# First attention pair loaded as f32 by two other queues, shorter VectorE steps, whole-array summary scores, and a planner with measured times

## The chip, the cores and the metric

The kernel runs on one core of one Trainium2 chip. The core has five engines with instruction streams of their own: TensorE (PE, its weight loads are shown as PEld), VectorE (DVE), ScalarE (ACT), GpSimd (POOL) and SyncE (SP), and 16 DMA engines that all of the core's queues share. Matrix products are written to PSUM, which has eight banks; everything else lies in SBUF. The time that counts is the device time of one execution in microseconds, median of the runs. In the lines of the profile, L12 means line 12 of the kernel before.

## What is computed

Two stages follow each other. The first is a sparse attention with 4 batches, 8 heads, 768 positions and head size 64: each query sees the keys less than 16 positions away, and 24 summaries of blocks of 32 keys.

```python
k_sum = k.reshape(B, H, nb, block, D).max(axis=3)      # block = 32, nb = 24
v_sum = v.reshape(B, H, nb, block, D).mean(axis=3)
scores_l = where(|i - j| < 16, scale * q @ k.T, -1e9)
scores_s = scale * q @ k_sum.T + log(block)
a = softmax(concat[scores_l, scores_s]);  x = a @ concat[v, v_sum]
```

The second is a mixture of 8 experts over the 3072 rows of x (512 wide), hidden size 1024. The gate's weights P are normalised eight times by rows and by columns over all rows, and the output is the sum of the experts weighted by P.

```python
P = exp(x @ w_gate - max)
for _ in range(8):
    P /= P.sum(1, keepdims=True) + 1e-9
    P /= P.sum(0, keepdims=True) + 1e-9
    P *= N / E
out = sum_e P[:, e:e+1] * (relu(x @ w1[e]) @ w2[e])
```

## The kernel before, in words

**Tiling.** Attention works on 16 pairs of heads, four pairs to a batch. Pair i belongs to batch i // 4. The two heads of a pair lie on partitions 0 to 63 and 64 to 127 of the transposed tiles `kT` and `qT`. Batch 0 is done in halves of 384 positions (`pair_half`), the other batches as whole pairs (`pair_whole`). For each pair: keys, queries and values are loaded by POOL's queue with a cast to bf16 (`load_qk`, `load_qh`, `load_v`); keys and queries are transposed on PE (`tr`, `tr_qh`, L312 to L315 and L299) and copied out of PSUM by ACT or DVE (L204); from pair 12 on the transposes are DMAs on SP's queue (`tr_dma`, L320). `key_max` (L338) takes the maxima of 32 keys, `block_sums` (L354) the sums of values by a product with the constant `m_blk`, and `block_out` (L361) copies them into the diagonal blocks of `V_s` or `V_e`. `scores` and `scores_h` (L344) make the local scores, `summaries` and `summaries2` (L432, L442) the summary scores, as products of 64 rows and 32 columns, one per head. ACT takes exponentials (L389, L452, L469), DVE multiplies by the band mask, PE makes the weighted values (L418 to L424, L492 to L507), DVE divides by the sums (`normalize`, L520 and L521), and `to_xT` or, for pairs 10 to 14, a DMA transpose (`x_dma`, L324) brings the result into `xT`. `near_values` copies edge rows of the values by four small DMAs on SP's queue.

**Expert 0** is computed in eight parts of 384 rows as soon as its rows of `xT` and its weights are there (L208 `hidden_mm`, L218 `project_mm`). It fills the time that attention leaves on PE. Experts 1 to 7 come after it in an order written out by hand (the loop over `groups`, from L1217), which the change does not touch.

**What sets the order.** For attention, expert 0, the gate's eight turns (`bridge`, L1120) and the first four groups of expert 1, a planner writes the order. Each step is a `Unit` with an engine (or a choice of two), a cost in us, the steps it depends on, a priority, and PSUM buffers that it opens or uses. `Plan.order` (L58) keeps a clock per engine, adds `HOP` (0.15) between engines and `RESHAPE` (0.1) when PE's tile shape changes, and emits the step that can start first. PSUM banks of a kind ("m" three, "a" three, "s" one double bank) are taken in turn, as a ring. A step's `lag` is the time after its end until others may use it; loads and DMA transposes have planned lags. Where the plan leaves PE idle before the first evacuation of expert 0, it inserts filler products of zeros (`keep_busy`, L566). The plan decides the order of instructions alone; on the chip each engine runs its list in order and waits on semaphores.

**At the front**: POOL's queue issues pair 0's keys, queries and values, makes the identity, issues pair 1's keys and queries, makes the band mask (two operations that wait for DVE's memset of `band`, L585), and goes on with pair 1's values, pairs 2 and 3, expert 0's weights and the later batches. DVE sets the constants (`constants`, L595) meanwhile; `pads` (L589) clears the gaps in the tiles `Eh`.

Of the kernel before, what the change touches and what calls it, by code (L numbers as in the profile page):

```python
# [34 lines left out]
class Plan:  # L35

    HOP = 0.15
    RESHAPE = 0.1

    def __init__(self, slots, idle=None):  # L40
        self.slots, self.idle, self.shape = {}, idle, None
        self.ring, self.turn, self.free, self.waiting = {}, {}, {}, []
        self.more(slots)

    def more(self, slots):
        for t, n in slots.items():
            self.slots[t], self.ring[t], self.turn[t] = n, [None] * n, 0
# [10 lines left out]
    def order(self):  # L58
        free, ring, turn, waiting = self.free, self.ring, self.turn, self.waiting
        left = []  # L60

        def ready(u):
            t = 0.0
            for i, b in enumerate(u.opens):
                old = ring[b.tag][(turn[b.tag] + i) % self.slots[b.tag]]
                if old is not None:
                    if any(x.start is None for x in old.users):
                        return None
                    t = max([t] + [x.end + (self.HOP if x.on not in u.eng else 0.0) for x in old.users])
            return t  # L70

        while waiting or left:
# [4 lines left out]
            for u in left:  # L77
# [3 lines left out]
                for e, cost in u.eng.items():  # L81
                    if e == "PE" and u.shape != self.shape:
                        cost += self.RESHAPE
                    t = max([t0, free.get(e, 0.0)]
                            + [d.end + d.lag + (self.HOP if d.on != e else 0.0) for d in u.deps])
# [8 lines left out]
            if self.idle is not None:  # L94
# [3 lines left out]
                while self.idle is not None and t > free.get("PE", t) + us:  # L98
# [10 lines left out]
                    ring["m"][turn["m"] % self.slots["m"]] = x.opens[0]  # L109
                    turn["m"] += 1  # L110
                    yield x
            u.start, u.end, u.on = t, end, e
# [3 lines left out]
            for b in u.opens:  # L116
                ring[b.tag][turn[b.tag] % self.slots[b.tag]] = b
                turn[b.tag] += 1
            left.remove(u)
            yield u  # L120
# [3 lines left out]
def kernel(  # L124
# [23 lines left out]
    W = 16  # L148
# [86 lines left out]
    if True:  # L235
# [4 lines left out]
        m_blk = attn.tile([128, G, 128], BF16, name="m_blk")  # L240
        qT = [attn.tile([128, W + S + W], BF16, name=f"qT{i}") for i in range(NB)]
        kT = [attn.tile([128, S], BF16, name=f"kT{i}") for i in range(NB)]
        ksT = [attn.tile([128, 32], BF16, name=f"ksT{i}") for i in range(NB)]
# [14 lines left out]
        def bank(tag, name, dtype=FP32):  # L258
            pool, n = (mps, 3) if tag == "m" else (aps, NA)
            return pool.tile([128, 2048 // mybir.dt.size(dtype)], dtype, tag=tag, name=name, bufs=n)  # L260

        def banks2(name, dtype=FP32):
            return aps.tile([128, 2, 2048 // mybir.dt.size(dtype)], dtype, tag="s", name=name, bufs=NS)
# [1056 lines left out]
```

## Time and profile before

| what | value |
|---|---|
| median of 3 runs | 676.51 us (675.13 to 679.61) |
| the profiled execution's own time | 676.52 us |
| its span in the profile | 674.8 us |
| PE busy | 660.7 us (98%), 5107 matmuls |
| DVE busy | 578.9 us (86%) |
| ACT busy | 404.6 us (60%) |
| POOL busy | 132.6 us (20%) |
| granted TensorE clock | 0.999 |
| chain that ended last | PE 88%, DMA 5%, DVE 4% |

The profile is one execution. Busy is the time in which an engine had an instruction in work; matmuls are pipelined, so that a busy PE can still be waiting a little between them. Besides the page, the trace behind it can be asked for the instructions of a stretch in order of time, for busy time by stretch, for the waits and what ended them, and for the chain of work that ended last, followed back from the last instruction.

### The profile page before, as it was taken

The numbers are of one execution on the slowest core, as the hardware profiler recorded it, in microseconds if no ns is written. First come the engines' busy times: TensorE is split into PE (matmuls) and PEld (weight loads), VectorE is DVE, ScalarE is ACT, GpSimd is POOL, SyncE is SP. The second block draws the span as 40 slices with busy tenths as digits, with TensorE's granted clock in tenths as the row PEclk, the third lists the DMA queues.
The fourth block names the chain that finished last, engine by engine and source line by source line (L and its number), as shares of the span: only waits on it lengthen the run. The fifth ranks groups of instructions, "written<-read, shape, count | busy, mean of one in ns | idle before, by whom it ended". The sixth has DMA issues, their size and how long they took to land.

```text
span 674.8 us, 13527 instructions
## 1 busy us (share of the span) xinstructions
PE 660.7 (98%) x5107; PEld 434.0 (64%) x5107; DVE 578.9 (86%) x1434; ACT 404.6 (60%) x787; POOL 132.6 (20%) x177
## 2 busy tenths in 40 slices
PE   8899998999999999999999999999999999999996
PEld 4566655555666666666666666666666666666665
DVE  7778896776799988998799988998899879998885
ACT  5678885565777765555655565555555565556551
POOL 8599631121101010201010010101020101100001
PEclk9999999999999999999999999999999999999999
DMA  9999999000513050311422051306031232201224
GB/s 119 187 145 146 135 117 154 1 1 1 79 11 37 1 79 1 36 13 23 57 23 27 1 78 11 39 1 79 1 34 16 25 55 23 26 1 53 88 80 157
DMA packets 124018, 36.46 MB, mean 54 GB/s; under 512 B 110384, under 2 KB 121136, under 8 KB 123952
## 3 DMA queue, kind: packets, MB, share of 16 engines
q0 software_dynamic: 104672, 26.22, 43.4%
q1 hardware_dynamic: 18464, 8.83, 6.7%
q8 instruction: 40, 0.66, 0.4%
q10 hardware_dynamic: 816, 0.54, 0.2%
q14 instruction: 26, 0.21, 0.1%
HBM read 52.45 MB, written 6.29 MB: 87 GB/s over the span
## 4 chain that ended last, share of the span: by engine, by line
PE 88%; DMA 5%; DVE 4%; POOL 1%; issue 1%; ACT 0%; DVEq 0%; ACTq 0%
PE xy L939 36%; PE pg L933 16%; PE pb L933 11%; PE pa L933 10%; PE yps L218 5%; PE hps L208 4%; DMA xT<-xs 2%; DMA qst<-in_q_dram 2%; DMA w<-in_moe_w_dram 1%; PE sg L344 1%; PE tkq L315 1%; DVE xs L521 1%; PE vs L354 1%; PE tx L528 0%; DVE hf L883 0%
## 5 line engine op out<-in xcount | busy, mean ns | idle before, releaser
L939 PEld LDWEIGHTS <-hf 128*128 128x128 f16 x2352 | 230.1, 98 | 96.9 <-issue 2.3
L939 PE MATMUL xy<-w,hf 128*128 128x256 f16 x1312 | 183.4, 273 | 0.1
L939 PE MATMUL xy<-ws,hf 128*128 128x256 f16 x984 | 147.6, 273 | 0.4
L199 ACT ACTIVATE hf<-pg 128x512 f16<-128x512 f32 x84 | 50.2, 597 | 150.4 <-PE pg L933 150.4
L1075 DVE SCALAR_TENSOR_TENSOR out_acc<-xy,P_sb,out_acc 128x512 f32<-128x512 f32 x164 | 115.0, 742 | 1.7 <-PE xy L939 1.7
L880 DVE TENSOR_TENSOR hf<-hf 128x512 f16<-128x512 f16 x252 | 99.8, 423 | 8.8
L933 PE MATMUL pa<-xT,w 128*128 128x512 f16 x336 | 99.9, 379 | 0.0
L933 PEld LDWEIGHTS <-w 128*128 128x128 f16 x672 | 65.8, 98 | 43.8 <-issue 0.2
L883 DVE TENSOR_TENSOR hf<-pb,c 128x512 f16<-128x512 f32 x84 | 58.1, 691 | 38.8 <-PE pb L933 35.0
L184 POOL DMA_DIRECT2D w<-in_moe_w_dram x56 | 41.7, 756 | 221.1 <-PE pg L933 192.4
L933 PEld LDWEIGHTS <-ws 128*128 128x128 f16 x504 | 49.3, 98 | 25.3
L967 ACT COPY c<-pg 128x512 f32<-128x512 f32 x84 | 49.3, 586 | 22.4 <-PE pg L933 22.4
L883 DVE TENSOR_TENSOR hf<-pg,c 128x512 f16<-128x512 f32 x84 | 57.1, 679 | 0.7 <-PE pg L933 0.7
L952 ACT COPY pg<-pa 128x512 f32<-128x512 f32 x84 | 47.9, 570 | 4.8
L199 ACT ACTIVATE hf<-pa 128x512 f16<-128x512 f32 x84 | 50.6, 602 | 0.0
L960 ACT COPY c<-pb 128x512 f32<-128x512 f32 x84 | 49.7, 592 | 0.7 <-PE pb L933 0.5
L933 PE MATMUL pg<-xTs,w 128*128 128x512 f16 x168 | 50.0, 379 | 0.1
L933 PE MATMUL pg<-xTs,ws 128*128 128x512 f16 x168 | 50.0, 379 | 0.0
L933 PE MATMUL pb<-xT,ws 128*128 128x512 f16 x168 | 50.0, 379 | 0.0
L933 PE MATMUL pg<-xT,w 128*128 128x512 f16 x168 | 50.0, 379 | 0.0
L933 PE MATMUL pb<-xTs,ws 128*128 128x512 f16 x168 | 50.0, 379 | 0.0
L208 PE MATMUL hps<-xT,w 128*128 128x384 f16 x256 | 48.9, 326 | 0.0
(143 smaller groups left out, 819.6 us busy)
## 6 DMA issues: line engine op xcount, KB each, us to landing
w<-in_moe_w_dram POOLq DMA_DIRECT2D x8, 1024.0 KB, 9.0
w<-in_moe_w_dram POOLq DMA_DIRECT2D x56, 128.0 KB, 3.6
out_dram<-out_acc SPq DMA_DIRECT2D x20, 256.0 KB, 2.0
qst<-in_q_dram POOLq DMA_DIRECT2D x32, 96.0 KB, 6.0
vx<-in_v_dram POOLq DMA_DIRECT2D x16, 192.0 KB, 6.6
kst<-in_k_dram POOLq DMA_DIRECT2D x24, 96.0 KB, 6.2
w<-in_moe_w_dram POOLq DMA_DIRECT2D x2, 512.0 KB, 8.7
kst<-in_k_dram POOLq DMA_DIRECT2D x4, 192.0 KB, 4.9
```

Source lines behind the costliest of these rows:

```text
L184: nc.gpsimd.dma_start(out=t[:, :, h, :], in_=moe_w1[e].rearrange("(dk p) f -> p dk f", p=128)[:, :, f:f + 128])
L199: nc.scalar.activation(out=out, in_=in_, func=AF.Relu, bias=0.0, scale=1.0)
L208: nc.tensor.matmul(hp[:, 0:n], lhsT=w1s[e][:, dk, 128 * f:128 * (f + 1)], rhs=xT[:, dk, t0:t0 + n], start=(dk == 0), stop=(dk == KD - 1))
L218: nc.tensor.matmul(yp[:], lhsT=h[:, f, c * 128:(c + 1) * 128], rhs=w2s[e][:, f, :], start=(f == 0), stop=(f == KF - 1))
L880: nc.vector.tensor_tensor(out=out, in0=in0, in1=in1, op=ALU.subtract)
L883: nc.vector.tensor_tensor(out=out, in0=in0, in1=in1, op=ALU.add)
L933: nc.tensor.matmul(bank[:], lhsT=w[:, dk, :], rhs=x[:, dk, :], start=start and dk == 0, stop=dk == KH - 1, skip_group_check=True)
L939: nc.tensor.matmul(bank, lhsT=a(f)[:, 128 * c:128 * (c + 1)], rhs=w[:, f, :], start=start and f == 0, stop=f == FH - 1, skip_group_check=True)
L952: nc.scalar.copy(out=B["g"][:], in_=B["a"][:])
L960: nc.scalar.copy(out=B["c5"][:], in_=B["b"][:])
L967: nc.scalar.copy(out=B["c2"][:], in_=B["g"][:])
L1075: nc.vector.scalar_tensor_tensor(out=acc, in0=src, scalar=P_sb[:, t, e:e + 1], in1=acc, op0=ALU.mult, op1=ALU.add)
```

## The change

- **Pair 0's keys and first query half** are loaded as f32 by two queues other than POOL's: keys of head 0 and the queries by SP's, keys of head 1 by ACT's (`first_f32`), into tiles that later hold exponentials. ACT and DVE cast them to bf16 (`first_k`, `first_q`). POOL's queue starts with the identity and pair 0's values.
- **Constants**: the band's memset moves to the front of DVE's list, the Es tiles are cleared by ACT, `m_blk` is one shifted window of 148 columns instead of six blocks of 128, the V_s memsets are regrouped, the casts of the identity and the gate's weights come after pair 0's key maxima (`gate_constants`). A constant `own` holds ones where a head's own partitions are. The pads of the second and third Eh tile come later.
- **key_max** takes the maximum of two halves twice (32 to 16 to 8), reduces the rest, and multiplies by `own` into a block-diagonal `ksT` of 128 columns. **block_out** is one product with `own` instead of two copies.
- **Summary scores** are one product on 128 rows and 128 columns per half, for both heads, instead of one of 64 rows and 32 columns per head; `summaries2` goes.
- **Planner**: a bank is taken from those that are free first, not in turn; the time between engines is 0.23 after PE and 0.1 otherwise; costs and lags have new values.

The diff, cut to its core:

```diff
-    HOP = 0.15
+    HOP = {"PE": 0.23}
...
         def ready(u):
-            t = 0.0
-            for i, b in enumerate(u.opens):
-                old = ring[b.tag][(turn[b.tag] + i) % self.slots[b.tag]]
-                if old is not None:
-                    if any(x.start is None for x in old.users):
-                        return None
-                    t = max([t] + [x.end + (self.HOP if x.on not in u.eng else 0.0) for x in old.users])
+            t, u.slots = 0.0, []
+            for b in u.opens:
+                at = []
+                for n, old in enumerate(ring[b.tag]):
+                    if (b.tag, n) in u.slots or old is not None and any(x.start is None for x in old.users):
+                        continue
+                    at.append((max([0.0] + [x.end + hop(x, "PE") for x in old.users]) if old else 0.0, n))
+                if not at:
+                    return None
+                t0, n = min(at)
+                u.slots.append((b.tag, n))
+                t = max(t, t0)
             return t
...
-        ksT = [attn.tile([128, 32], BF16, name=f"ksT{i}") for i in range(NB)]
+        ksT = [attn.tile([128, 128], BF16, name=f"ksT{i}") for i in range(NB)]
+        own = attn.tile([128, 2, 26], BF16, name="own")
...
+        def first_f32():
+            at["kf"] = attn.tile([128, 2, 2 * LIVE * G // 4], FP32, tag="er", name="kf", bufs=2)
+            at["qf"] = attn.tile([128, 2, G * 64], FP32, tag="em", name="qf", bufs=2)
+            rows = k[0, 0:2].rearrange("j (p g) d -> p j (g d)", g=G)
+            for j, eng in ((0, nc.sync), (1, nc.scalar)):
+                eng.dma_start(out=at["kf"][:, j, 0:G * D], in_=rows[:, j, :])
+            nc.sync.dma_start(out=at["qf"][:, :, 0:HG * D],
+                              in_=q[0, 0:2, 0:HS].rearrange("j (p g) d -> p j (g d)", g=HG))
...
+        def first_k(eng, j):
+            copy(eng, at["st", 0, 0][:, j].rearrange("p g d -> p (g d)"), at["kf"][:, j, 0:G * D])
+
+        def first_q(eng):
+            copy(eng, at["st", 0, 1][:, 0].rearrange("p j g d -> p j (g d)"), at.pop("qf")[:, :, 0:HG * D])
+            at.pop("kf")
...
         def key_max(i):
             r = i % NB
-            nc.vector.tensor_reduce(out=ksT[r][:, 0:24],
-                                    in_=kT[r][:].rearrange("p (n w) -> p n w", w=32),
-                                    axis=AX.X, op=ALU.max)
+            km = attn.tile([128, 1, 24], BF16, tag="km", name="km", bufs=2)
+            half = attn.tile([128, 24, 16], BF16, tag="kh", name="kh", bufs=1)
+            rows = kT[r][:].rearrange("p (n w) -> p n w", w=32)
+            nc.vector.tensor_tensor(out=half[:], in0=rows[:, :, 0:16], in1=rows[:, :, 16:32], op=ALU.max)
+            nc.vector.tensor_tensor(out=half[:, :, 0:8], in0=half[:, :, 0:8], in1=half[:, :, 8:16], op=ALU.max)
+            nc.vector.tensor_reduce(out=km[:, 0, :], in_=half[:, :, 0:8], axis=AX.X, op=ALU.max)
+            nc.vector.tensor_tensor(out=ksT[r][:, 0:64].rearrange("p (j n) -> p j n", j=2)[:, :, 0:24],
+                                    in0=km[:].to_broadcast([128, 2, 24]), in1=own[:, :, 0:24], op=ALU.mult)
...
-            for j in range(2):
-                nc.vector.tensor_copy(out=dst[32 * j:32 * j + 32, j * VD:j * VD + D],
-                                      in_=vs[32 * j:32 * j + 32, j * D:(j + 1) * D])
+            nc.vector.tensor_tensor(
+                out=dst[0:64].rearrange("p (j x) -> p j x", j=2)[:, :, 0:D],
+                in0=vs[0:64].rearrange("p (j d) -> p j d", j=2),
+                in1=own[0:64, :, 24:25].to_broadcast([64, 2, D]), op=ALU.mult)
...
-            for j in range(2):
-                p0 = 64 * j
-                nc.tensor.matmul(ss[32 * j:32 * j + 32, 0:HS], lhsT=ksT[r][p0:p0 + 64, :],
-                                 rhs=qT[r][p0:p0 + 64, W + h * HS:W + (h + 1) * HS],
-                                 start=True, stop=True)
+            nc.tensor.matmul(ss[:, 0:HS], lhsT=ksT[r][:], rhs=qT[r][:, W + h * HS:W + (h + 1) * HS],
+                             start=True, stop=True)
...
-        nc.vector.memset(zeros, 0.0)
-        nc.vector.memset(ident, 0.0)
-        keep_busy(10)
+        nc.vector.memset(ident, 0.0)
+        nc.vector.memset(zeros, 0.0)
+        first_f32()
+        keep_busy(8)
...
             for t in E_s:
-                nc.vector.memset(t[64:128, :, :], 0.0)
+                nc.scalar.copy(out=t[64:128, :, :], in_=zeros[64:128, None, :].to_broadcast([64, HG, 128]))
...
-            U[key] = add("LAND", 0, None, [last[1]], lag=0.4)
+            U[key] = add("LAND", 0, None, [last[1]], lag=1.0 if late else 0.4)
...
-                                                        [U["kq"[z], i]] + (war_k, war_q)[z], prio, lag=5.0)
+                                                        [U["kq"[z], i]] + (war_k, war_q)[z], prio, lag=5.5)
...
-            clear = add("DVE", 0.65, lambda: pads(n), [c0], prio - 0.5) if 0 < n < NEH else None
+            clear = add("DVE", 0.65, lambda: pads(n), [U["km", n - 1]], prio - 0.2) if 0 < n < NEH else None
...
             U["near", i] = add("SP", 2.5, lambda: near_values(i), [U["v", i], U.get(("A", i - NE, 1))], prio,
-                               lag=1.9)
+                               lag=4.5)
...
                 U["xt", i] = U["x", i] = add("SP", 1.25, lambda: x_dma(i), [U["no", i, 0], U["no", i, 1]], prio,
-                                             lag=4.5)
+                                             lag=6.5)
...
-        load_pair(0, "k0v")
         U["ident"] = last[0] = add("POOL", 0.35, ident_constant, [last[0]])
+        c0 = add("DVE", 3.1, constants, [], -5.0)
+        kf = add("LAND", 0, None, [], lag=4.0)
+        qf = add("LAND", 0, None, [], lag=4.5)
+        kc = [add("ACT", 0.46, lambda: first_k("ACT", 0), [kf], -4.0), add("DVE", 0.46, lambda: first_k("DVE", 1), [kf, c0], -4.0)]
+        U["k", 0] = add("LAND", 0, None, kc)
+        U["q", 0, 0] = add({"ACT": 0.46, "DVE": 0.46}, 0, lambda: first_q(U["q", 0, 0].on), [qf, c0, *kc], -4.0)
+        load_pair(0, "v")
         load_pair(1, "k0")
...
-                    step = add(eng, us, fn, [step], -50.0, opens=o, uses=w, lag=(1.2 if n else 2.0) if fn is columns else 0.0)
+                    step = add(eng, us, fn, [step], -50.0, opens=o, uses=w, lag=0.7 if fn is columns else 0.0)
```

Most other changed lines are planned costs: 0.95 to 0.85 for `key_max`, 0.36 to 0.24 and 0.84 to 0.70 for `block_out`, 0.4 to 0.5 (batch 0) and 0.335 for the transposes, 0.22 and 0.18 to 0.17 for the summary scores, and similar small steps. As built, PE's list has 5107 matmuls before and 30 fewer after (32 summary products for 64, 24 fillers for 22).

## The prediction

> **What bounds the kernel now.** I read the busy time by stage first, cut where the work changes: attention of batch 0 (0 to 35 us), attention of batches 1 to 3 over expert 0 (to 120), the eight normalisation turns of the gate over the rest of expert 0 and the first groups of expert 1 (to 172.8). The columns are the stretch, its length, then busy time of PE, PEld, DVE, ACT and POOL, the granted clock, DMA share and GB/s.
>
> ```profile
> core 0: us, PE busy (x) PEld busy (x) DVE busy (x) ACT busy (x) POOL busy (x), PEclk, DMA share, GB/s
> 0.00:10.00 10.00, 7.53 (x67) 3.50 (x67) 7.44 (x66) 3.77 (x5) 8.06 (x16) 1.00 1.00 93
> 10.00:20.00 10.00, 9.03 (x161) 6.13 (x156) 8.78 (x23) 7.47 (x11) 9.02 (x12) 1.00 1.60 165
> 20.00:35.00 15.00, 13.14 (x192) 8.40 (x189) 10.80 (x34) 9.46 (x17) 8.47 (x10) 1.00 1.71 185
> 35.00:100.00 65.00, 64.85 (x771) 40.40 (x770) 57.03 (x153) 53.28 (x85) 47.08 (x59) 1.00 2.09 136
> 100.00:120.00 20.00, 17.41 (x187) 10.25 (x188) 14.54 (x46) 10.39 (x20) 3.44 (x5) 1.00 1.37 137
> 120.00:172.80 52.80, 52.80 (x304) 28.23 (x302) 36.52 (x92) 31.73 (x63) 13.16 (x19) 1.00 0.04 4
> ```
>
> PE is full from 35 to 100 us and from 120 on. It is empty for 35 - 29.70 = 5.30 us of the first 35 and for 20 - 17.41 = 2.59 us between 100 and 120. Part of the "busy" of the first 35 us is filler. The same view for the filler line alone (stretch, length, PE busy):
>
> ```profile
> 0.00:10.00 10.00, 5.44 (x15) 1.60 (x15) 1.00 1.00 93
> 10.00:20.00 10.00, 1.68 (x6) 0.52 (x7) 1.00 1.60 165
> 20.00:35.00 15.00, 0.49 (x2) 0.00 (x0) 1.00 1.71 185
> ```
>
> So of 172.8 us, at most 5.30 + 7.61 + 0.15 + 2.59 = 15.7 us are not useful PE work. Everything behind 172.8 us (502 us) stands in the same order in both programs: PE's last 3481 matmuls are the same. The change can win only from these 15.7 us and from the length of its own matmuls, and a microsecond won early reaches the end whole, because expert 0 fills every later gap. What holds the two weak stages is in the chain of work (start, length, what) and in the list of waits (total, times, longest):
>
> ```profile
> 7.18 0.99 POOL vx L284
> ...
> 12.94 7.66 DMA w<-in_moe_w_dram
> ...
> 22.50 11.39 DMA qst<-in_q_dram
> ...
> 101.33 15.10 DMA xT<-xs x2
> ```
> ```profile
> PE lp L542 <- DMA xT<-xs: 1.6, 1, 1.6
> ...
> PE sg L344 <- DVE qT L204: 1.0, 1, 1.0
> ...
> PE tx L528 <- DVE xs L521: 0.7, 2, 0.4
> ```
>
> Early it is the loads on POOL's queue, up to pair 4's queries (issued 21.7, used 34.03); late it is the transposes by DMA.
>
> **Part 1, loads of pair 0.** Two issues leave the head of POOL's queue: 0.95 (keys, at 1.29) and 0.74 us (queries). The wait of the band mask goes too:
>
> ```profile
> 6.48 0.31 POOL L577 TENSOR_SCALAR_AFFINE_SELECT band<-band 128x160 bf16<-128x160 bf16 x1 [0.69 <-DVE band L585]
> ```
>
> Its memset now stands at the front of DVE's constants. By the durations of the same rows (identity 0.33, values 1.04, keys and queries 0.74 each, masks 0.69, from 1.29 on) the second values issue moves from 7.12 to about 4.85: 2.3 us. The bytes are as many as before, and the DMA share is over 1.3 from 10 us on, so issuing earlier helps only if the engines had room. They had: the share in the first 5 us is 0.50. I bound what reaches pair 4 by 0 and 2.3 us. The Trainium skill (DMA: Bandwidth & Descriptors, Issuing engines are not separate DMA queues) says that transfers of all issuing engines run on the same 16 engines and interleave, so that spreading them saves issue time alone. By that rule 1.7 us of issue would be the most. The share of 0.50 speaks against reading it as "nothing"; from 10 us on the trace agrees with it.
>
> Pair 0 itself is not sooner. The f32 transfers should be there by about 3.5 us (the 256 KB stores on SP land 2.0 us after issue, the 16 KB gate weights 1.9). But half of the keys is cast on DVE behind the constants. Those run from 1.32 to 5.45 now; the new list loses 0.56 (Es), 0.28 (m_blk's size), 0.3 (four memsets) and about 0.5 (gaps between memsets of one tile) and gains 0.19 (band), 0.34 (whole ksT) and 0.35 (own): it ends near 4.7. With a cast of 0.5 (qT copy 128x384: 0.53) the transposes start near 5.2, against 5.18. DVE is what is late next. SP has nothing else before 35.9 us, so its two issues delay nobody; ACT's cast, query cast and two Es copies (four of some 0.48) fall into its idle 2.99 us before 5.75.
>
> **Part 2, DVE of batch 0.** DVE is busy 13.93 us of 5 to 21.4, so its order is the engine chain there. Query copy 0 waits behind pads and band until 6.97; in the new order it is next after the cast. The scores then wait for ACT's key copy (5.75 + 0.80) and start near 6.6 instead of 7.52. The pads (0.6) and the gate casts (0.48) now stand before the first masks, which start near 8.8 instead of 9.30. So 0.5 to 0.9 us there. Per pair, block_out changes from two casts of 0.214 to one product; the nearest rows are 0.19 (32x80) and 0.25 on the line from 0.167 (32 elements) to 0.549 (768): 0.2 us less. key_max (0.947) becomes four instructions. On the same line: 384 elements 0.35, 192 elements 0.25, a 192-element reduce 0.34, a small product 0.17: 1.11. Consecutive DVE starts overlap by some 0.08 (0.28 us instructions every 0.20), so 0.85; ends 0.85 and 1.11, which is -0.1 to +0.17 per pair. I take -0.1, nearest to the overlapped rows. By pair 3 that is 0.5 to 0.9 plus 3 x 0.3, about 1.5 us. In the later stages DVE's gain lies beside a full PE and is worth nothing.
>
> Loads allow up to 2.3, DVE about 1.5; both are needed, so I take **-1.5** (from 0 to -2.3).
>
> **Part 3, new lags and banks.** The waits of 100 to 120 us are 1.57 (logits of batch 2 for a DMA transpose), 0.40 + 0.35 (transposes waiting for normalize, itself 1.85 behind a DMA transpose) and 0.27 (near rows): 2.59. The planner counted 1.25 + 4.5 for an x transpose; the trace has a median of 6.8 to landing, highest 7.9. It now counts 7.75. In the new order 68 + 48 matmuls of expert 0 stand between the second and third logits instead of 60 + 32. At 0.163 and 0.216 (0.65 and 0.86 for four) that is 4.8 us more cover against a wait of 1.57. Free choice of banks can only remove planned waits, but the rebuilt order may meet new ones. Bounds: -2.59 and +1; I take **-2.0**.
>
> **Part 4, summary scores.**
>
> ```profile
> 39.41 0.27 PE ss L442 x4
> ...
> 34.53 0.65 PE hps L208 x4
> ```
>
> Four tiled matmuls of 384 columns take 0.27; two whole ones by the second row 0.33. Twelve pairs: +0.7. Batch 0: eight times 0.163 for about 0.24, -0.6, but half of them beside filler or idle PE, so -0.3. Sum **+0.4** (0 to +0.9). The Trainium skill (TensorEngine Tiling (Array Packing), Key Properties) says that a change of tiling mode drains the array; no row shows a drain by itself, and by it the +0.4 would shrink.
>
> Two fillers fewer ahead cost nothing: they end at about 4.5 instead of 4.7, ahead of transposes that wait until 5.2.
>
> **Sum**: 676.52 (own time of the profiled run: span 674.8 and 1.7 around it; the median of the runs is 676.51) - 1.5 - 2.0 + 0.4 = **673.4 us**. The three runs lie between 675.13 and 679.61, so about 1% is what can be told from no change.
>
> **Rivals.**
> *Nothing comes through.* The transfers share their engines (the rule of the page cited in Part 1, read strictly), pair 4's queries land at 34 us as before, and the new order trades one wait for another: 676.5 + 0.4 = 676.9. For it: DMA share of 1.6 and 1.7 from 10 to 35 us. Against it: half-empty DMA engines up to 5 us, and 2.59 us of waits with a named cause.
> *Slower: the gate's turns run out of cover.* Behind the last logits the new order leaves 88 + 72 matmuls of expert 0 instead of 96 + 88, 4.8 us less. Between successive column totals PE has 4.6 to 5.9 us of work (mean 5.1), where the totals now come every 5.79 us (126.38 to 166.90). From one total to the end of the next column sums the trace has 3.2 to 4.5 us, so the cover just suffices. It decides from a turn of about 4.6 on: if DVE's queue lets a turn take 5.8, PE waits 7 x 0.7 = 4.8 us: 678.2.
> *More.* The load stream comes through whole (-2.3), all waits of 100 to 120 go (-2.6), matmuls cost nothing, and planned bank waits of about 1 us go: 670.6.
>
> **Chances.** Forecast 0.52, nothing 0.22 (676.9), slower 0.13 (678.2), more 0.13 (670.6). Range 670.5 to 678.3: it takes in all four. Faster by over 1% (below 669.7) needs more than every term's far end: 0.05. Slower by over 1% (above 683.3) needs turns of 6.5 us or a new wait of 10: 0.07. Within 1%: 0.88.
>
> **What would show it.** Right: second values issue near 4.9, first transposes near 5.2, first scores near 6.6, pair 4's query transposes near 32.3, PE over 19 of 20 us between 100 and 120, first product of expert 1's second layer some 3 us sooner, an identical course behind it. Wrong: pair 4 at 34 again, PE waits at the gate's totals, or the PE gaps of 100 to 120 merely moved.

## The result, and the profile after

| | kernel before | changed kernel |
|---|---|---|
| median of 10 executions each | 676.57 us (675.13 to 679.61) | 671.46 us (670.13 to 674.88) |
| ratio of the times | 1 | 0.9925, 95% interval 0.9908 to 0.9942 |
| profiled execution's own time, its span | 676.52, 674.8 us | 674.88, 673.2 us |
| first product of expert 1's second layer | 168.77 us | 168.53 us |

The changed kernel is 5.1 us faster by the medians, 0.75%, where -3.1 was forecast; it lies inside the range and inside 1%. The profiled execution of the changed kernel happened to be the longest of its ten, 3.4 us above their median, and this must be kept in mind while reading its profile: some 4.5 us of it belong to an event that most executions don't have, or have smaller. A second series of the same kernel gave 672.35 us, 3.8 us below the kernel before in that series (676.18). Differences below about 1 us between two series are therefore not told apart here.

Busy time by stage in the changed kernel, with the same cuts and columns as before (stretch, length, then busy time of PE, PEld, DVE, ACT and POOL, granted clock, DMA share, GB/s):

```profile
core 0: us, PE busy (x) PEld busy (x) DVE busy (x) ACT busy (x) POOL busy (x), PEclk, DMA share, GB/s
0.00:10.00 10.00, 8.23 (x74) 3.71 (x75) 7.22 (x67) 6.22 (x10) 8.95 (x17) 1.00 1.22 151
10.00:20.00 10.00, 9.48 (x157) 6.26 (x154) 9.49 (x34) 6.15 (x9) 7.33 (x10) 1.00 1.63 178
20.00:35.00 15.00, 14.88 (x234) 10.81 (x232) 12.46 (x38) 11.60 (x21) 9.99 (x13) 1.00 1.84 180
35.00:100.00 65.00, 64.27 (x714) 40.06 (x711) 57.94 (x174) 46.28 (x76) 46.38 (x59) 1.00 1.88 134
100.00:120.00 20.00, 16.86 (x164) 9.98 (x163) 15.18 (x51) 9.60 (x18) 1.36 (x2) 0.93 1.15 126
120.00:172.80 52.80, 52.80 (x312) 28.68 (x310) 35.72 (x90) 32.06 (x62) 12.12 (x19) 1.00 0.04 5
```

The filler line alone (stretch, length, PE busy, PEld busy):

```profile
0.00:10.00 10.00, 5.81 (x14) 1.53 (x14) 1.00 1.22 151
10.00:20.00 10.00, 3.15 (x10) 0.81 (x10) 1.00 1.63 178
20.00:35.00 15.00, 0.00 (x0) 0.00 (x0) 1.00 1.84 180
```

Three things stand in these rows. From 20 to 35 us PE went from 13.14 busy us to 14.88, none of it filler: the early stage is where the gain is. Up to 20 us busy time without filler is 8.75 us now and was 9.44: nothing was won there by this measure. And from 100 to 120 us, where 19 of 20 busy us were forecast, PE has 16.86, less than the 17.41 of before, at a mean clock of 0.93.

The chain of work that ended last (start, length, what) shows both stages:

```profile
1.46 5.31 DMA vx<-in_v_dram
6.81 0.50 PE vs L393 x6
7.32 0.35 PE sg L383 x8
...
8.79 0.66 DVE Eh L503
...
31.47 0.34 PE tkq L349 x6
...
33.28 0.34 PE tkq L349 x6
...
104.56 11.35 DMA Ve<-vx
115.91 0.14 issue
116.04 0.40 PE av L464 x3
```

In the kernel before pair 4's keys and queries (the products `tkq` near 33 us) came after waits for their loads, at 32.73 and 34.03 (start, length, engine, line, operation, and in brackets the idle time before it and what ended it):

```profile
32.73 0.49 PE L315 MATMUL tkq<-ident,kst 128*128 128x128 bf16 x6 [0.46 <-DMA kst<-in_k_dram]
34.03 0.50 PE L315 MATMUL tkq<-ident,qst 128*128 128x128 bf16 x6 [0.81 <-DMA qst<-in_q_dram]
```

Now they come at 31.47 and 33.28, and no wait stands before them. In the late stage the DMA transposes of x are gone from the chain. In their place stand the edge rows of the last pair's values (`Ve`), issued at 104.56 and landing 11.35 us later. The list of PE's waits up to 172 us (total, times, longest) begins with it:

```profile
PE av L464 <- DMA Ve<-vx: 2.9, 1, 2.9
...
PE tx L554 <- DVE xs L547: 0.3, 1, 0.3
```

Behind this wait the clock falls. The same view by stage, cut finer:

```profile
114.00:116.00 2.00, 0.00 (x0) 0.00 (x0) 0.64 (x4) 0.00 (x0) 0.00 (x0) 1.00 0.90 132
116.00:118.00 2.00, 1.96 (x17) 1.17 (x18) 1.45 (x5) 0.00 (x0) 0.00 (x0) 0.77 0.02 3
118.00:120.00 2.00, 2.00 (x9) 0.90 (x8) 1.93 (x9) 0.59 (x1) 0.00 (x0) 0.50 0.00 0
120.00:122.00 2.00, 2.00 (x13) 1.07 (x11) 2.00 (x7) 1.37 (x2) 0.00 (x0) 0.88 0.00 0
```

Half clock for 0.92 + 2.0 + 0.48 = 3.4 us costs 1.7 us of full-speed work. With the 2.9 us of the wait that is 4.6 us in this one execution.

### The profile page after: what moved, and what is told of

Read it like the earlier page. It is cut to its first block, busy times and chain, and to the rows that moved or that the text cites. A ratio compares the mean times of both kernels' runs of the same rounds, so it can differ in the third digit from the quotient of the medians.

```text
span 673.2 us, 13510 instructions
## 1 busy us (share of the span) xinstructions
PE 661.4 (98%) x5077; PEld 436.4 (65%) x5077; DVE 581.9 (86%) x1475; ACT 399.7 (59%) x782; POOL 129.5 (19%) x175
## 4 chain that ended last, share of the span: by engine, by line
PE 88%; DVE 6%; DMA 5%; issue 0%; ACT 0%; DVEq 0%; ACTq 0%
PE xy L978 37%; PE pg L972 16%; PE pa L972 11%; PE pb L972 11%; PE yps L231 5%; PE hps L221 4%; DMA Ve<-vx 3%; DMA kT<-kst 1%; DVE xs L547 1%; DMA vx<-in_v_dram 1%; PE sg L383 1%; PE tkq L349 1%; PE tx L554 0%; DVE km L377 0%; PE vs L393 0%
## 6 DMA issues: line engine op xcount, KB each, us to landing
Ve<-vx SPq DMA_DIRECT2D x48, 10.2 KB, 4.6
```

## The experiments

For the stage sums below I measured PE from start to start: a matmul is charged the distance to the next matmul's start, up to about 1.3 times what its width usually takes, and the rest of the distance counts as idle. The kernels held in the order of the changed one have the same sequence of steps, so that only the edit differs.

### The changed kernel again

> The changed kernel once more. Its profiled run took 674.88 us, its median is 671.46, and that profile shows a 2.9 us wait of PE for the near-rows DMA at 113 us, after which the granted clock was 0.50 for 3.4 us (1.7 us lost). Theory A: that wait is an accident of that one execution; another profile shows less than 1 us of it, no half clock, a time within 1 us of 671.5, and PE over 18.5 of 20 us busy from 100 to 120. Rival B: the wait is in every run, and the profiled time is again near 674.

Measured: 672.35 us (670.83 to 675.69), ratio 0.9945 (0.9928 to 0.9962). The profiled execution was again the longest of its series, with the same event:

```profile
PE av L464 <- DMA Ve<-vx: 3.9, 1, 3.9
```

So the late wait is no accident of one execution, but the median shows that it is not typical either.

### The three f32 transfers on POOL's queue

```diff
-            for j, eng in ((0, nc.sync), (1, nc.scalar)):
+            for j, eng in ((0, nc.gpsimd), (1, nc.gpsimd)):
...
-            nc.sync.dma_start(out=at["qf"][:, :, 0:HG * D],
+            nc.gpsimd.dma_start(out=at["qf"][:, :, 0:HG * D],
```

> As changed, in the same order of all compute instructions, but pair 0's three f32 transfers are issued by POOL's queue, ahead of the identity. Theory (queue): POOL's later issues move back by three issues of some 0.7 us, about 2 us; the second values issue stands near 7 us, and the time is 1.5 to 2.3 us above the changed kernel. Rival (same 16 DMA engines, so only bytes count): within 0.4 us of the changed kernel.

Measured: 673.69 us (672.27 to 674.63), ratio 0.9967 (0.9955 to 0.9978), 1.3 us behind the changed kernel's second series, run beside it; the intervals just overlap. Not all of it need be the queue's: six of the ten executions here have a mean granted clock of 0.996 or 0.997, two of ten did in that series. The chain of work says more than the median:

```profile
3.72 4.46 DMA vx<-in_v_dram
8.22 0.50 PE vs L393 x6
8.72 0.35 PE sg L383 x8
...
32.88 0.34 PE tkq L349 x6
...
34.69 0.34 PE tkq L349 x6
```

The first scores come 1.40 us later than in the changed kernel (7.32), and pair 4's keys and queries both 1.41 later (31.47 and 33.28). An issue moved at the head of the load stream shifts the whole of batch 0 rigidly; how much of the 1.4 us arrives at the end is not settled by the medians. The three issues take 2.1 us on POOL. The bytes, their form and their destination are the same.

### The steps of VectorE as before

```diff
-            nc.vector.tensor_tensor(out=half[:], in0=rows[:, :, 0:16], in1=rows[:, :, 16:32], op=ALU.max)
-            nc.vector.tensor_tensor(out=half[:, :, 0:8], in0=half[:, :, 0:8], in1=half[:, :, 8:16], op=ALU.max)
-            nc.vector.tensor_reduce(out=km[:, 0, :], in_=half[:, :, 0:8], axis=AX.X, op=ALU.max)
+            nc.vector.tensor_reduce(out=km[:, 0, :], in_=rows, axis=AX.X, op=ALU.max)
...
-            nc.vector.tensor_tensor(
-                out=dst[0:64].rearrange("p (j x) -> p j x", j=2)[:, :, 0:D],
-                in0=vs[0:64].rearrange("p (j d) -> p j d", j=2),
-                in1=own[0:64, :, 24:25].to_broadcast([64, 2, D]), op=ALU.mult)
+            for j in range(2):
+                nc.vector.tensor_copy(out=dst[32 * j:32 * j + 32, j * VD:j * VD + D],
+                                      in_=vs[32 * j:32 * j + 32, j * D:(j + 1) * D])
```

> As changed, same order, but key_max is one reduce of 768 elements and the product with own, and block_out is two copies again. Theory (DVE sets batch 0): four pairs times some 0.3 to 0.4 us, so 1.0 to 1.6 us above the changed kernel. Rival (DVE's steps lie beside the loads and a full PE): within 0.4 us.

Measured: 673.06 us (672.38 to 673.35), ratio 0.9954 (0.9939 to 0.9969): 0.7 us behind the changed kernel's 672.35, with overlapping intervals, so not told from nothing by time. The instructions in order of time tell more. Pair 1 in the changed kernel (start, length, engine, line, operation):

```profile
9.92 0.35 DVE L375 TENSOR_TENSOR kh<-kT 128x384 bf16<-128x384 bf16 x1
10.30 0.26 DVE L376 TENSOR_TENSOR kh<-kh 128x192 bf16<-128x192 bf16 x1
10.60 0.35 DVE L377 TENSOR_REDUCE km<-kh 128x24 bf16<-128x192 bf16 x1
10.98 0.18 DVE L378 TENSOR_TENSOR ksT<-km,own 128x48 bf16<-128x48 bf16 x1
...
11.78 0.28 DVE L399 TENSOR_TENSOR Vs<-vs,own 64x128 bf16<-64x128 f32 x1
```

and pair 1 with the old steps:

```profile
9.80 0.94 DVE L374 TENSOR_REDUCE km<-kT 128x24 bf16<-128x768 bf16 x1
10.78 0.18 DVE L375 TENSOR_TENSOR ksT<-km,own 128x48 bf16<-128x48 bf16 x1
...
11.58 0.44 DVE L397 CAST Vs<-vs 32x64 bf16<-32x64 f32 x2
```

From the first instruction of `key_max` to the next one's start the medians over 16 pairs are 870 ns in the kernel before (one reduction), 1088 with reduction and product, and 1166 with the four steps. The four steps are **longer** than what they replace, by 0.30 us, of which the product with `own`, which the whole-array scores need, is 0.22. `block_out` is shorter: 473 ns before, 201 to 243 in batch 0 where something is queued behind it. So a pair costs DVE about as much as before (+0.03 to +0.07 us in batch 0), and DVE's busy time over the kernel even rose, from 578.9 to 581.9 us.

### The summary scores in tiles, in the places of the whole ones

```diff
-            nc.tensor.matmul(ss[:, 0:HS], lhsT=ksT[r][:], rhs=qT[r][:, W + h * HS:W + (h + 1) * HS],
-                             start=True, stop=True)
+            for j in range(2):
+                p0 = 64 * j
+                nc.tensor.matmul(ss[32 * j:32 * j + 32, 0:HS], lhsT=ksT[r][p0:p0 + 64, 32 * j:32 * j + 32],
+                                 rhs=qT[r][p0:p0 + 64, W + h * HS:W + (h + 1) * HS],
+                                 start=True, stop=True)
```

> As changed, same order, but the summary scores are again two products of 64 rows and 32 columns per half. By the rows of before (0.27 us for four against 0.33 for two whole ones, batch 0 half hidden) 0.4 us faster than the changed kernel. Rival (changing the tile shape costs time around the product): 0.5 to 1.5 us slower than the changed kernel.

Measured: 673.14 us (672.34 to 674.65), ratio 0.9959 (0.9945 to 0.9973), 0.8 us behind the changed kernel, intervals overlapping. From start to start two tiled products take 269 ns and are preceded by some 95 ns more than usual when the neighbour uses the whole array; one whole product takes some 170 ns, mostly with under 10 ns before it when the neighbour is whole too. Summed over all summary scores with what precedes them: 7.66 us in the kernel before, 7.93 in the changed one, 10.65 here. So 2.7 us more of PE's time came out as some 0.8 us of run time, which is itself not told from nothing: PE time of these products is not run time one for one. The kernel before was cheap because it put four tiled products in a row (69 ns each), which this experiment doesn't.

### The summary scores in tiles, planned anew

The same edit, and the planner told of it: cost 0.22 and a tile shape of their own.

```diff
-                U["ss", i, h] = add("PE", 0.17, lambda h=h: summaries(i, h, "a"),
-                                    [U["km", i], U["kT", i, 1], U.get(("A", i - NE, 1))], prio, opens=[buf])
+                U["ss", i, h] = add("PE", 0.22, lambda h=h: summaries(i, h, "a"),
+                                    [U["km", i], U["kT", i, 1], U.get(("A", i - NE, 1))], prio, opens=[buf],
+                                    shape="tile")
...
```

> The changed kernel with the summary scores as two products of 64 rows and 32 columns per half again, and this time with the planner told so (their cost of 0.22 and their tile shape as in the kernel before), so that it may put them beside other work of small tiles. The forecast's price of +0.4 for whole-array products says: 671.5, some 0.3 us faster than the changed kernel. Rival 'a change of tile shape costs more than the products save': 672.5 to 673.2, as when the tiled ones were put in the places of the whole ones (+0.8).

Measured: 675.61 us (674.92 to 677.04), ratio 0.9993 (0.9982 to 1.0004): 3.3 us behind the changed kernel, which neither theory had. The scores take 10.94 us here, much as when held in place. PE's useful time up to the first product of expert 1's second layer is 150.1 us against 147.7 where nothing else disturbs the changed order. So 2.4 us are PE's own work; the rest is not explained by one wait. What can be said is that two tiled products per half won nothing against one whole product in either placement (0.8 us slower in place, which is not told from nothing, and 3.3 us planned anew), and that this isn't the form that the kernel before had.

### Lags: old ones in the changed kernel, new ones in the kernel before

```diff
-            U[key] = add("LAND", 0, None, [last[1]], lag=1.0 if late else 0.4)
+            U[key] = add("LAND", 0, None, [last[1]], lag=0.4)
...
                     U["tr", i, z] = U["kT", i, z] = add("SP", 1.25, lambda z=z: tr_dma(i, z),
-                                                        [U["kq"[z], i]] + (war_k, war_q)[z], prio, lag=5.5)
+                                                        [U["kq"[z], i]] + (war_k, war_q)[z], prio, lag=5.0)
...
             U["near", i] = add("SP", 2.5, lambda: near_values(i), [U["v", i], U.get(("A", i - NE, 1))], prio,
-                               lag=4.5)
+                               lag=1.9)
...
                 U["xt", i] = U["x", i] = add("SP", 1.25, lambda: x_dma(i), [U["no", i, 0], U["no", i, 1]], prio,
-                                             lag=6.5)
+                                             lag=4.5)
```

> As changed, but planned with the old lags (near rows 1.9, key and query transposes 5.0, x transposes 4.5, late loads 0.4); the order is made anew. Theory (the lags took away the waits of 100 to 120 us): 1.5 to 2.6 us above the changed kernel, with waits for DMA transposes back. Rival (the new lags only moved the waits): within 0.7 us.

Measured, old lags in the changed kernel: 673.89 us (671.05 to 675.54), ratio 0.9955 (0.9934 to 0.9977). The wait that the new lags were to remove is back in PE's list, and the clock halves behind it (stages, 102 to 104 us):

```profile
PE lp L568 <- DMA xT<-xs: 2.0, 1, 2.0
```

```profile
102.00:104.00 2.00, 2.00 (x20) 1.06 (x18) 1.75 (x5) 0.76 (x2) 0.00 (x0) 0.50 1.63 152
```

How the difference goes with the clock can be read from the ten executions, since each has its mean granted clock: the four with 0.998 to 1.000 took 671.05 to 671.89 us, as long as the changed kernel; the six with 0.993 to 0.997 took 673.39 to 675.54. Of the twenty executions of the changed kernel three lie at 0.997 or below. So the median moves by how often an execution has the wait with the fallen clock behind it; what the wait and the clock each cost is not separated by these times.

The reverse: the kernel before with the new lags alone, in which PE's order changes from 32 us on.

> The kernel before, planned with the new lags and nothing else changed. Theory (lags): 1.5 to 2.6 us below the kernel before. Rival: within 0.7 us of it.

Measured: 676.75 us (674.79 to 679.72), ratio 1.0003 (0.9986 to 1.0021): nothing. Its waits:

```profile
PE av L424 <- DMA Ve<-vx: 3.5, 2, 3.1
```

The logits no longer wait, and pair 11's edge rows now do, for 3.1 us at 87 us, with half clock behind it in the profile and a mean of 0.995 to 0.997 in all ten executions. One wait was traded for another. Early it did win: useful PE work up to 35 us is 21.8 us against 20.05, because the planner, told of later landings, puts other work ahead of pair 4's transposes. From 35 to 100 us the idle time then rises from 2.05 to 6.4 us.

### The last weights behind the last edge rows

Expert 1's second weights (one transfer of 1 MB, on POOL's queue) are issued at 100.40 us in the changed kernel, just ahead of the last pair's edge rows on SP's. Here a copy of one element on POOL holds them until those rows have landed. PE's order is the same.

```diff
+        def hold_near():
+            nc.gpsimd.tensor_copy(out=held[0:1, 0:1], in_=V_e[(NP - 1) % NE][96:97, 0, VD:VD + 1])
+        last[0] = add("POOL", 0.3, hold_near, [last[0], U["near", NP - 1]])
         load("w2n", lambda: load_w2(1), 0.85, 5.0)
```

> As changed, but POOL issues the load of expert 1's second weights (1 MB) only after the last near rows have landed (it copies one of their elements first). Two profiles of the changed kernel have PE waiting 2.9 and 3.9 us near 113 us for near rows that were issued at 104.6, while these weights flow on POOL's queue. Theory (contention): the wait falls below 0.8 us, no half clock, and the median falls by 1 to 3 us against the changed kernel. Rival (the near rows are late behind the DMA transposes of their own queue): the wait stays, time within 0.5 us of the changed kernel.

Measured: 670.87 us (669.84 to 671.28), ratio 0.9921 (0.9895 to 0.9946). The trace in order of time, PE's and POOL's instructions:

```profile
109.85 0.28 POOL L891 COPY held<-Ve 1x1 bf16<-1x1 bf16 x1 [9.73 <-DMA Ve<-vx]
110.32 0.89 POOL L208 DMA_DIRECT2D w<-in_moe_w_dram  x1 [0.19 <-issue]
```

```profile
112.89 0.34 PE L464 MATMUL av<-Ve,Ee 128*128 128x130 bf16 x3
```

The edge rows, last issued at 104.06, are there by 109.85, in under 5.8 us instead of 11.35. PE doesn't wait for them at all, and the clock stays full as long as PE works. A shorter wait is new: the held weights now flow beside the last transposes of x, and at 120.59 us the logits wait for one of these.

```profile
PE lp L568 <- DMA xT<-xs: 1.0, 1, 1.0
```

Nothing but the weights' place in time was changed, so the late landing is put down to the transfer of the weights beside it; this rests on one profile here and two of the changed kernel. By what path the weights delay the rows is not separated. On SP's queue a transpose of x is issued just ahead of the rows, and the rows land behind it: it lands at 112.49 in the changed kernel and at 108.88 here. In the four profiles where the issue of this transpose starts behind that of the weights (by 0.1 to 1.1 us) it takes 11.2 to 12.6 us to land, in the ten where it starts ahead of them 4.0 to 10.4. In the changed kernel the two issues stand 0.36 us apart (100.40 and 100.76), which may be why its executions differ; no run tested that by itself. The gain in the median is small, probably because few executions of the changed kernel have the wait in full.

### Filling the gap

The kernel before with the new lags, and 44 small products of zeros where PE stood idle for 3.15 us:

```diff
+            for _ in range(44 if (i, h) == (11, 0) else 0):
+                nc.tensor.matmul(av[:, 400:512], lhsT=zeros[:], rhs=zeros[:, 0:112], start=False, stop=False,
+                                 skip_group_check=True)
```

> This is the kernel before with the new lags alone, with the identical order of work, and 44 small products of zeros (112 columns, into columns of the same bank that nobody reads) put where PE stood idle for 3.15 us before pair 11's near product. The near rows still come when they come. Theory 'the idle gap takes the clock': the granted clock stays at 1.0 behind the gap, and the 3.4 us of half clock, worth 1.7 us, go: about 675.0 against 676.75 without the fillers. Rival 'the half clock costs nothing, or comes from something other than the idle time': clock still 0.5 for 3.4 us or the time unchanged, 676.5 to 677. If the fillers outlast the wait by more than 0.3 us, the time is longer by that much, and the line of waits no longer shows the near rows.

Measured: 677.28 us (675.31 to 679.29), ratio 1.0015 (1.0003 to 1.0026). The clock did stay at 1.0 behind pair 11, with a rest of 1.0 us in the wait. But it fell 15 us later, behind a wait of only 1.3 us:

```profile
PE lp L545 <- DVE xs L524: 1.3, 1, 1.3
```

```profile
106.00:108.00 2.00, 2.00 (x6) 0.44 (x3) 1.92 (x6) 0.00 (x0) 0.00 (x0) 0.50 1.75 115
```

The first half of the theory (the idle gap takes the clock) is supported by this one profile, the second (so the fill is worth 1.7 us) failed.

### First scores ahead of the first block sums

In the changed kernel PE's first scores were queued behind the block sums, which wait for the values' DMA. Here the two are exchanged, and nothing else.

```diff
+            if u is U["vs", 0]:
+                held_unit = u, plan.now
-            if u.fn is not None:
+            elif u.fn is not None:
                 u.fn()
+            if u is U["S", 0, 0]:
+                plan.now = held_unit[1]
+                held_unit[0].fn()
```

> The changed kernel with one exchange: pair 0's block sums stand behind its first scores on PE instead of ahead of them; all else in the same order. Theory 'DVE's chain of batch 0 bounds, so an earlier first score is worth time': scores start near 6.5 instead of 7.25, the first masks at 8.5 instead of 8.79 (the pads end at 8.4), and some 0.3 us reach the end: about 671.6, against 671.5 to 672.4 for the changed kernel itself, which is hard to tell, so the useful PE work up to 35 us is the better witness: 23.0 plus 0.3. Rival 'the loads bound batch 0': the scores start earlier, and the useful work up to 35 us stays at 23.0 within 0.1.

Measured: 671.64 us (670.79 to 672.01), ratio 0.9932 (0.9920 to 0.9945). The instructions in order of time:

```profile
6.65 0.39 PE L383 MATMUL sg<-qT,kT 64*128 64x160 bf16 x8
...
7.40 0.50 PE L393 MATMUL vs<-vx,m_blk 128*128 128x128 bf16 x6 [0.35 <-DMA vx<-in_v_dram]
...
8.93 0.59 DVE L503 TENSOR_TENSOR Eh<-erh,band 128x960 bf16<-128x960 bf16 x1
```

The scores start 0.6 us sooner, and the masks start later than before (8.93 against 8.79), because on DVE they stand behind `block_out`, which waits for those block sums. Useful PE work up to 35 us: 22.9 us, as in the changed kernel (23.0). The rival's figure came out. But the masks did not start sooner, so the theory's own condition was not met: earlier scores alone bring nothing while `block_out` stands ahead of the masks. That the loads set batch 0 is shown by the run with the transfers on POOL's queue. The profiled execution of this kernel has only 0.6 us of the late wait and a full clock, so it shows what the changed order does in an ordinary execution.

### Banks in turn, and the best version

```diff
-                for n, old in enumerate(ring[b.tag]):
+                k = (self.turn.get(b.tag, 0) + seen.get(b.tag, 0)) % len(ring[b.tag])
+                seen[b.tag] = seen.get(b.tag, 0) + 1
+                for n, old in ((k, ring[b.tag][k]),):
...
```

> As changed, but PSUM banks are taken in turn again, with the new times and lags; the order is made anew (17 fillers instead of 24). Theory (banks chosen free are worth little, since PE is full from 35 us on): within 0.7 us of the changed kernel. Rival (waits for the next bank in turn held PE's order back): 1 to 3 us above it.

Measured: 671.06 us (669.46 to 674.03), ratio 0.9931 (0.9907 to 0.9955): the free choice of banks wins nothing that shows. In the order that comes of it expert 1's second weights are issued at 105.29 us, behind the last edge rows (104.09), and these land 5.2 us later, which agrees with the run before. One of its six executions still took 674.03 us at a mean clock of 0.995. With both edits, banks in turn and the weights held:

> The changed kernel with banks taken in turn as before, and with the 1 MB of expert 1's second weights issued behind the landing of the last pair's near rows. Theory 'what is left of the new order's loss is the race of the near rows against those weights': the wait for the near rows and the half clock go in every run, median 670.3 to 670.9 and no run above 672.5. Rival 'the two edits win the same microsecond': the median stays where each alone has it, 670.9 to 671.1, with the same spread of 4 us.

Measured: 669.77 us (669.49 to 670.10), ratio 0.9908 (0.9893 to 0.9923), 6.7 us faster than the kernel before and 1.7 us below the lower of the changed kernel's two medians, with a spread of 0.6 us over four executions; the changed kernel's was 4.8 over ten. PE's stage of 100 to 120 us is full:

```profile
100.00:120.00 20.00, 20.00 (x213) 12.18 (x212) 15.37 (x50) 11.12 (x22) 7.79 (x11) 1.00 1.18 139
```

## Why the prediction was right, and where its terms were not

The stage sums from start to start, in us. "Ordinary" is the kernel with the first scores ahead, whose time of 672.01 in the profiled execution lies near the changed kernel's medians. Useful is PE work without filler:

| | before | changed, profiled | ordinary | last weights held | best |
|---|---|---|---|---|---|
| useful PE work up to 35 | 20.05 | 22.95 | 22.87 | 23.05 | 22.08 |
| idle 35 to 100 | 2.05 | 3.00 | 2.62 | 2.63 | 1.89 |
| idle 100 to 125 | 3.31 | 4.30 and half clock | 2.33 | 1.92 | 0.24 |
| first product of expert 1's second layer | 168.77 | 168.53 | 165.33 | 164.82 | 162.80 |
| from there to the end of the span | 506.0 | 504.6 | 505.0 | 504.7 | 504.9 |

By the "ordinary" column the span changes by -2.8 (early) + 0.6 (35 to 100) - 1.0 (100 to 125) - 0.2 (shorter work behind) - 1.1 (tail) = -4.5 us, which is the difference of the spans (674.8 to 670.3).

Direction and range were right, and so was the place of the gain, the two weak stages. That the sum came near is in part luck: up to 100 us the change brought 0.8 us more than forecast, behind it 1.0 us less, and the two cancel. The tail's 1.1 us is not shown to belong to the change (see below); without it the profiles say -3.4, against -3.1 forecast and -5.1 by the medians.

**Part 1, loads, and Part 2, VectorE (forecast -1.5 together; measured -2.3 by 100 us).** The sign and place were right, its inner account was wrong. The prediction's step "loads allow up to 2.3, DVE about 1.5; both are needed, so I take -1.5" fails. The load stream came through: the second values issue stands at 4.84, forecast 4.85,

```profile
4.14 0.35 POOL L604 TENSOR_SCALAR_AFFINE_SELECT band<-band 128x160 bf16<-128x160 bf16 x1
...
4.84 1.03 POOL L318 DMA_DIRECT2D vx<-in_v_dram  x1
```

expert 0's first weights are issued at 10.65 instead of 12.94, pair 4's keys at 19.40 instead of 20.88, and the 0.46 and 0.81 us that PE waited for pair 4's loads are gone. All of the gain lies between 20 and 35 us, where 11.5 useful us became 14.3. Loads and lags overlap in it: with old lags the changed kernel still has 23.0 useful us by 35, with POOL's queue 21.6, and the kernel before with new lags 21.8 instead of 20.05. What either alone brought to the change is therefore not told apart. DVE had no share of the forecast kind: the term "3 x 0.3" took 0.2 from `block_out`, which did save that much (473 to 201 or 243 ns), and 0.1 from pricing `key_max` at 0.85 against 0.947, and it takes 1.17 against 0.87 from start to start. The four durations were right (0.35, 0.26, 0.35 and 0.18, forecast 0.35, 0.25, 0.34 and 0.17). What failed is the overlap: each of the four needs the one before, so that each starts some 0.03 us after its end and not 0.08 ahead of it, while the single reduction did overlap its independent successor by 0.08, and I had charged it in full. The first scores at 6.6 failed too (7.25): I had looked at what the scores need and not at what is queued ahead of them on PE, the block sums that wait for the values until 6.81. That miss cost nothing, since scores at 6.65 brought no earlier masks. The masks came at 8.79, forecast 8.8; the first transposes at 4.79, forecast 5.2; pair 4's query transposes at 33.28, forecast 32.3, but without a wait.

The Trainium skill (DMA: Bandwidth & Descriptors, Issuing engines are not separate DMA queues) would have spreading save issue time alone. The trace agrees with it: putting the three issues back on POOL's queue, 2.1 us of issue, shifts batch 0 by 1.4 us. What the prediction made of it as a rival, that nothing comes through, is not in the rule: issue time at the head of the stream is not small here.

**Part 3, lags and banks (forecast -2.0; measured -1.0 in the late stage).** The mechanism was half right. The logits and transposes wait no longer for x: the 1.57, and of the 0.40 + 0.35 all but 0.3, are gone in the changed kernel's profile, and old lags bring the logits' wait back (2.0). With the first scores ahead the transposes wait 0.43 + 0.35, much as before, and with the weights held the logits wait 1.0, so the new lags do not remove these waits from every execution. The step that failed is "the rebuilt order may meet new ones. Bounds: -2.59 and +1": the new order drew the last edge rows into the transfer of expert 1's weights, and a wait of 2.9 us with 1.7 us of clock behind it is 4.6 us, far over the bound of +1. It decided the profiled execution, where "19 of 20" became 16.86, and not the median; a sign that the prediction had named as wrong, that the gaps of 100 to 120 merely moved, was there in both profiles of the changed kernel. Nor are the lags worth anything by themselves: in the kernel before they trade a wait of 1.57 for one of 3.1. The free choice of banks is worth nothing that shows.

**Part 4, summary scores (forecast +0.4; measured +0.28).** By the prediction's own measure, PE time of these products with the change of shape before them, the term was right; in run time no experiment shows it, since 2.7 us of such PE time came out as only some 0.8 us. The drain that no row of the kernel before showed by itself is now visible as some 95 ns in front of a tiled product beside a whole one; as the prediction said of the Trainium skill's page (TensorEngine Tiling (Array Packing), Key Properties), this makes the term smaller than 0.4.

**The tail** was forecast as identical. The order is, but the profile of before loses 1.1 to 1.4 us there in six distances between matmuls that are about 0.24 us longer than usual, three of them 146 us apart; the others show none to three. The two other kernels with the order of before, the one with new lags and the one with the filled gap, have none of them and take 504.2 us from the same product to the end. So the 506.0 is not the price of the order of before, and what makes these distances is open.

**The gate's turns** did not run out of cover: from 120 to 172.8 us PE is full in the changed kernel too. The slower rival had the wrong place; the real danger stood 10 us ahead of it. (Its 7 x 0.7 is 4.9, not 4.8.)

## What to carry to other kernels

An order of work that hides one transfer may put another one beside a long one: when a planner is given longer landing times, look at which small transfers now run beside the large ones, and place the large one behind them by a dependence, not by hope. Issues at the head of a serial load stream delay all that comes behind them: 2.1 us of them moved batch 0 by 1.4. Price a replaced instruction from its start to the next one's start on both sides, not one side by duration and the other by overlap.

## What the runs showed of the hardware

- A copy of edge rows of 10.2 KB on SP's queue took 11.35 us to land beside 128 KB and 1 MB weight transfers on POOL's, under 5.8 us when the 1 MB one was held back, and 6.1 us in the kernel before, where it was issued 5.3 us behind the same 1 MB. The DMA transpose of x ahead of the rows on SP's queue took 11.2 to 12.6 us where its issue started behind that of the 1 MB, and 4.0 to 10.4 where it started ahead (fourteen profiles).
- The granted clock fell to half for 3.4 us, once each, in five profiles of four kernels, after PE waits of 2.9, 3.9, 3.1, 2.0 and 1.3 us, and did not fall after waits of 1.57 in the profile of before and of 1.4 in that of the scores planned anew. The Trainium skill (TensorE: Matmul & The Clock Gate, Part 1: The HAM clock gate) tells of a free-running window of about 3.4 us, one idle window of which halves the clock. The length of the half-clock stretch agrees with the window; the length of the wait needed does not, since 1.3 and 2.0 us sufficed here. What a window counts as idle is not settled by these runs.
- On VectorE, splitting a reduction of 768 elements (0.95 us) into two maxima and a shorter reduction (0.35, 0.26, 0.35) saves nothing: with the product behind it 1166 ns from start to next start, against 1088 unsplit.
